# A recurrent attention kernel in which some TensorE operations are divided by columns until four steps hold exactly 2560 TensorE instructions

## The chip, the cores and the metric

The kernel runs on one core of one Trainium2 chip. The metric is the device time of one execution in microseconds, the median of several runs. A core has a matrix engine (TensorE, in the profile PE for its matmuls and PEld for its weight loads), VectorE (DVE), ScalarE (ACT), GpSimd (POOL) and SyncE (SP), which here only issues DMA. Each engine has an instruction stream of its own, and they wait for each other by semaphores.

## What is computed

Two branches over the same 2048 rows of 512 values, mixed row by row with a gate: attention that goes through the rows in 64 segments of 32 with a memory of 8 rows carried from each segment to the next, and a two-layer perceptron.

```python
for s in range(n_seg):                       # 64 segments of 32 rows
    xs = x[:, s * seg_len:(s + 1) * seg_len, :]
    h = jnp.concatenate([mem, xs], axis=1)   # 8 + 32 rows
    q = jnp.einsum('btd,dhe->bhte', h, Wq)   # 32 heads of 128
    k = jnp.einsum('btd,dhe->bhte', h, Wk)
    v = jnp.einsum('btd,dhe->bhte', h, Wv)
    scores = jnp.einsum('bhqe,bhke->bhqk', q, k) * scale
    p = softmax(where(mask, scores, -1e9))
    o = jnp.einsum('bhqk,bhke->bhqe', p, v)
    o = jnp.einsum('bhte,hed->btd', o, Wo)
    mem = o[:, :M, :]
    outs.append(o[:, M:, :])
...
h = gelu(jnp.einsum('bsd,df->bsf', layernorm(x), w1) + b1)
b = jnp.einsum('bsf,fd->bsd', h, w2) + b2
return g * a + (1 - g) * b
```

## The kernel before

A first stage of some 74 us loads the weights and computes the perceptron for all rows; for nine of the sixteen 128-row tiles its second layer is put off, and the hidden values go to DRAM. Then 64 *steps* follow, one for each segment, four to a *tile* of 128 rows (steps 0 to 3 are tile 0; `si` is the place of a step in its tile, 0 to 3). The memory makes the steps a chain: each needs the 8 rows that the one before it made.

A step on TensorE, in program order, with the lines that the profile names. A matmul of the projections has a 32-column stationary operand, so four of them stand side by side in the array and form a *group* of four; a *unit* is one such group for one of the four 128-row parts of the contraction.

- Query and key projection, 16 units of four 512-column matmuls (`qk_unit`, L128).
- Scores (L266, L270), 40 and 64 columns each, the value projection (`v_unit`, L147, 512 columns), and short sums in between (L277, L280, L701).
- `av` (L290, L295): 80 short matmuls of 40 or 64 columns.
- The output projection of the eight memory rows, `wo_pass`: eight groups of four 512-column matmuls (`wo_group`, L159).
- The new memory, `new_mem`: three blocks of 8-column matmuls (L746), each on a part of `w`, which ScalarE copies out of PSUM behind `wo_pass` (L737). VectorE then puts the result into the `hT` of the next step (L748).

In the waits of this chain TensorE does *side work* for another tile, handed out in units by a generator: `run(n)` takes the next n units of it. With `si` 0 and 1 that is the query and key projection for the last eight rows of each segment of the next tile (`left_qk`), with `si` 3 their value projection (`left_v`), with `si` 2 the output projection for such rows of the tile before (`wo_left`, eight `wo_group`s). Put-off perceptron work (L674, groups of four 256-column matmuls) is also taken in half units. In the steps with `si` 0 from tile 2 on, an output selection of two groups stands before `new_mem` (L229, L233). The numbers of units before `wo_pass`, behind it and between the blocks of `new_mem` stand in the table `WS` and in two further `run(1)`.

SyncE issues the DMA in program order. Once a step, behind `recip_x`, it writes the reciprocal sums to DRAM and reads them back as a broadcast to 128 partitions, `Rb` (512 KB); GpSimd scales the attention output with it in the next step (L730).

TensorE executes its instructions in exactly the order written (matmul, weight load and some waits each count as one). No planner moves them.

Of the kernel before, what the change touches and what calls it, by code (L numbers as in the profile page):

```python
# [28 lines left out]
def kernel(ctx, tc, A_x, A_mem0, A_Wq, A_Wk, A_Wv, A_Wo, A_seg_len, B_x, B_w1, B_b1, B_w2, B_b2, gate_w, out):  # L29
    nc = tc.nc  # L30
    P = 128
    _, S, Dm = A_x.shape
    H, Dh = A_Wq.shape[1], A_Wq.shape[2]
    M = A_mem0.shape[1]
    seg = int(A_seg_len)
    nseg = S // seg
    L = M + seg
    F = B_w1.shape[1]
    KC = Dm // P
# [22 lines left out]
    Wo_sb = pers.tile([P, H, Dm], BF16)  # L62
# [50 lines left out]
    X2 = lps.tile([P, 512], FP32)  # L113
    SbF = lps.tile([P, 512], FP32)
    W = lps.tile([P, 512], FP32)
# [5 lines left out]
    W5 = (Wq5, Wk5)  # L121
    Wv5 = Wv_sb[:].rearrange("p k (i j e) -> p k i j e", i=NG, j=4)
    HF = ((0, H // 2), (H // 2, H))

    def qk_unit(bk, G, t, hf, kc):
        h0, h1 = HF[hf]
        for j in range(4):
            nc.tensor.matmul(bk[32 * j:32 * j + 32, :], lhsT=G[:, kc, :], rhs=W5[t][:, kc, h0:h1, j, :],  # L128
                             start=(kc == 0), stop=(kc == KC - 1), tile_position=(0, 32 * j))

    def qk_cast(bk):
        Tb = ew.tile([P, 8, 32, 2], BF16, tag="Tb", bufs=3, name="Tb")
# [10 lines left out]
            nc.vector.transpose(out=dst, in_=Tb[:, jh:8:2].rearrange("p a e b -> p a (e b)").bitcast(FP32))  # L143

    def v_unit(bk, G, vb, kc):
        for j in range(4):
            nc.tensor.matmul(bk[32 * j:32 * j + 32, :], lhsT=G[:, kc, :], rhs=Wv5[:, kc, 4 * vb:4 * vb + 4, j, :],  # L147
                             start=(kc == 0), stop=(kc == KC - 1), tile_position=(0, 32 * j))

    def v_out(V, vb):  # L150
        return V[:, 4 * vb:4 * vb + 4, :].rearrange("p i e -> p (i e)")

    HORD = [(j, ih) for j in (0, 2, 1, 3) for ih in range(2)]

    def wo_group(bk, U_, n):
        j, ih = HORD[n]
        for c in range(4):
            i = 4 * ih + c
            nc.tensor.matmul(bk[32 * c:32 * c + 32, :], lhsT=U_[:, j, i, :], rhs=Wo_sb[:, 4 * i + j, :],  # L159
                             start=(n == 0), stop=(n == NW - 1), tile_position=(0, 32 * c))  # L160

    NW = len(HORD)

# [431 lines left out]
    UT = [lp.tile([P, 4, NG, 32], BF16, name=f"UT{i}") for i in range(2)]  # L595
# [14 lines left out]
    Rs = {}  # L610
    fill = iter(())

    def run(n):
        for _ in range(n):
            next(fill, None)

    def chain(*gens):
        for x in gens:
            yield from x
# [29 lines left out]
    def hm_load4():  # L649
        x = cw.tile([P, Dm], BF16, tag="c", name="c").rearrange("p (k t) -> p k t", k=KC)  # L650
        T, fc = work[0]
        nc.sync.dma_start(x[:], h_dr[T][:, fc:fc + KC])
        for k in range(KC):
            hms.append((*work.pop(0), x[:, k], 0))
# [74 lines left out]
            for h in range(2):  # L729
                nc.gpsimd.tensor_tensor(out=out[:, :, 4 * h:4 * h + 4, o:o + b - a], in0=XR[:, :, 4 * h:4 * h + 4, a:b], in1=Rb[:, h, :, :, a:b], op=ALU.mult)  # L730

    def wo_pass(U_, cuts=(0, Dm), bk=W):
        for n in range(NW):
            wo_group(bk, U_, n)
        w = cw.tile([P, Dm], BF16, tag="w", bufs=8, name="w")
        for a, b in zip(cuts, cuts[1:]):
            nc.scalar.copy(out=w[:, a:b], in_=bk[:, a:b])  # L737
        return w
# [9 lines left out]
        nc.vector.tensor_copy(out=hn[:, k0:k0 + nk, RIDE:32], in_=bk.rearrange("p (k m) -> p k m", k=nk))  # L748


    QK4 = ((0, 0), (1, 0), (0, 1), (1, 1))
    WS = ((2, 2, 1), (2, 2, 2), (2, 2, 2), (2, 2, 2))
    for s in range(nseg):
        T, si = divmod(s, SPT)
        last = s == nseg - 1
        hc, hn = hT[s % 3], hT[(s + 1) % 3]
        W1, W2, W3 = WS[si]
# [75 lines left out]
        if last:  # L833
            break
        run(W1)
        if s:
            next(mlp, None)
# [61 lines left out]
    wl, c = wls.pop(T), cs.pop(T)  # L899
# [160 lines left out]
```

## Time and profile before

| | |
|---|---|
| median of 3 runs | 754.07 us (753.94 to 754.29) |
| profiled execution, its own time | 755.67 us |
| its span in the profile | 753.8 us |
| mean granted TensorE clock | 0.998 of full |
| matmuls, and as many weight loads | 19,896 |
| TensorE instructions in a tile's four steps (tiles 2 to 14) | 609 + 601 + 601 + 601 = 2412 |

The profile's page gives the busy time and its share of the span for each engine, and a chain that is followed back from the last instruction: at each point to what released it. "issue" in that chain is time in which an engine waited for nothing that the profile shows. Matmuls overlap in the array, so the duration of one (0.38 us for 512 columns) is not its price: the price is read from how far apart groups start, as the chain of work shows it. A view by windows gives the busy time and count of each engine in stretches that one chooses; here the stretches go from the first matmul of one step to the first of another, or from inside one hole in TensorE's work to inside another. The DMA part names queues: q8 of the kind "instruction" carries instructions, not data.

### The profile page before, as it was taken

The page shows a single profiled execution, that of the slowest core. Times are in us where ns is not written, and L with a number is a line of the kernel's source. Part 1 is how long each engine was busy: PE and PEld are TensorE (multiplying, and loading weights), DVE is VectorE, ACT ScalarE, POOL GpSimd, SP SyncE. Part 2 cuts the span into 40 slices and gives each one's busy share as a digit, 9 for nine tenths or more (in the row PEclk, how much of TensorE's full clock was granted, in tenths as well). Part 3 has the DMA queues.
Part 4 walks back from the last instruction along what each step waited for, and adds up shares of the span by engine and source line. Part 5 has one row for each costly group of instructions (what it writes and reads, how often), then busy time and mean ns, then how long its engine had stood idle before and what let it go on. Part 6 is the DMA issues. An engine that isn't in the chain of part 4 may idle for free.

```text
span 753.8 us, 45384 instructions
## 1 busy us (share of the span) xinstructions
PE 736.0 (98%) x19896; PEld 429.8 (57%) x19896; DVE 399.5 (53%) x1415; ACT 535.6 (71%) x1627; POOL 274.2 (36%) x516
## 2 busy tenths in 40 slices
PE   8999999999999999999999999999999999999996
PEld 5776555555555555555555565555555655555553
DVE  6776555446454554445554545445464545555444
ACT  5777667777776776777777777767777777777663
POOL 4001323444324444334433344333443334433341
PEclk9999999999999999999999999999999999999999
DMA  9999323122321323221322313231323222222321
GB/s 312 343 335 362 104 85 87 55 76 72 93 77 46 91 70 96 69 83 53 92 77 80 86 46 93 68 96 67 70 72 86 79 72 78 57 90 74 95 70 37
DMA packets 69997, 77.17 MB, mean 102 GB/s; under 512 B 34873, under 2 KB 59938, under 8 KB 68258
## 3 DMA queue, kind: packets, MB, share of 16 engines
q1 hardware_dynamic: 68802, 72.65, 31.4%
q8 instruction: 157, 2.57, 1.4%
q0 software_dynamic: 448, 1.05, 0.5%
q10 hardware_dynamic: 544, 0.52, 0.3%
q14 instruction: 46, 0.38, 0.2%
HBM read 60.21 MB, written 7.70 MB: 90 GB/s over the span
## 4 chain that ended last, share of the span: by engine, by line
PE 91%; DVE 3%; DMA 2%; issue 2%; ACT 1%; POOL 0%; DVEq 0%; SPq 0%; ACTq 0%; POOLq 0%
PE U L128 33%; PE X L159 19%; PE X L147 17%; PE X L128 4%; PE U L290 3%; PE W L674 3%; PE U L147 2%; PE SbF L482 1%; PE U L266 1%; DMA xt<-in_A_x_dram 1%; PE W L482 1%; PE U L489 1%; DVE junk L465 1%; PE SbF L266 1%; PE SbF L701 1%
## 5 line engine op out<-in xcount | busy, mean ns | idle before, releaser
L730 POOL TENSOR_TENSOR UT<-XR,Rb 128x384 bf16<-128x384 bf16 x126 | 140.2, 1134 | 310.1 <-DMA Rb<-r_dr 252.6
L133 ACT CAST Tb<-U 128x512 bf16<-128x512 f32 x288 | 168.7, 586 | 78.7 <-PE U L128 72.5
L128 PEld LDWEIGHTS <-hT 128*32 128x32 bf16 x4096 | 108.9, 96 | 95.5 <-DVE hT L748 1.1
L147 PE MATMUL X<-Wv_sb,hT 128*32 128x512 bf16 x2048 | 144.9, 378 | 0.9 <-issue 0.9
L128 PE MATMUL U<-Wq_sb,hT 128*32 128x512 bf16 x2048 | 145.1, 380 | 0.0
L128 PE MATMUL U<-Wk_sb,hT 128*32 128x512 bf16 x2048 | 144.6, 379 | 0.0
L159 PE MATMUL X<-Wo_sb,UT 128*32 128x512 bf16 x2016 | 123.0, 380 | 0.2
L748 DVE CAST hT<-U 128x8 bf16<-128x8 f32 x126 | 21.0, 167 | 172.0 <-PE U L746 131.1
L811 ACT CAST V<-X 128x256 bf16<-128x256 f32 x256 | 88.7, 372 | 16.4 <-PE X L147 3.5
L137 DVE STREAM_TRANSPOSE QT<-Tb 128x256 f32<-128x256 f32 x128 | 57.0, 446 | 71.9 <-ACT Tb L133 71.5
L159 PEld LDWEIGHTS <-UT 128*32 128x32 bf16 x2048 | 56.6, 96 | 57.1 <-issue 17.7
L707 ACT CAST XR<-U 128x256 bf16<-128x256 f32 x252 | 78.6, 438 | 0.0
L737 ACT CAST w<-X 128x128 bf16<-128x128 f32 x189 | 44.8, 310 | 45.8 <-PE X L159 45.1
L137 DVE STREAM_TRANSPOSE KT<-Tb 128x256 f32<-128x256 f32 x128 | 57.0, 445 | 25.3 <-ACT Tb L133 25.3
L730 POOL TENSOR_TENSOR UL<-XR,Rb 128x128 bf16<-128x128 bf16 x126 | 60.2, 500 | 0.0
L147 PEld LDWEIGHTS <-hT 128*32 128x32 bf16 x2048 | 47.0, 94 | 22.3 <-issue 1.8
L842 ACT CAST UT<-U 128x64 bf16<-128x64 f32 x252 | 35.3, 227 | 28.2 <-PE U L295 28.2
L722 POOL TENSOR_TENSOR racc<-racc,R 128x72 f32<-128x72 f32 x63 | 21.2, 337 | 93.6 <-DVE R L720 49.9
L674 PE MATMUL W<-w_sb,hm 128*32 128x256 bf16 x728 | 52.7, 273 | 0.1
L794 ACT ACTIVATE E<-U 128x64 bf16<-128x64 f32 (+1 forms) x128 | 35.0, 273 | 11.3 <-PE U L270 11.1
L482 PEld LDWEIGHTS <-w_sb 128*128 128x128 bf16 (+1 forms) x352 | 33.5, 100 | 13.4 <-issue 2.4
L159 PE MATMUL X<-Wo_sb,UL 128*32 128x512 bf16 x512 | 39.8, 379 | 0.2 <-issue 0.2
(178 smaller groups left out, 1223.0 us busy)
## 6 DMA issues: line engine op xcount, KB each, us to landing
Rb<-r_dr SPq DMA_DIRECT2D x63, 512.0 KB, 3.9
Wv_sb<-in_A_Wv_dram SPq DMA_DIRECT2D x4, 1024.0 KB, 7.2
Wq_sb<-in_A_Wq_dram SPq DMA_DIRECT2D x4, 1024.0 KB, 8.5
Wk_sb<-in_A_Wk_dram SPq DMA_DIRECT2D x4, 1024.0 KB, 9.0
Wo_sb<-in_A_Wo_dram SPq DMA_DIRECT2D x4, 1024.0 KB, 9.7
VP<-VL SPq DMA_DIRECT2D x64, 64.0 KB, 3.2
hm<-h_dr SPq DMA_DIRECT2D x91, 32.0 KB, 2.2
c<-c_dr SPq DMA_DIRECT2D x16, 128.0 KB, 3.5
```

Source lines behind the costliest of these rows:

```text
L128: nc.tensor.matmul(bk[32 * j:32 * j + 32, :], lhsT=G[:, kc, :], rhs=W5[t][:, kc, h0:h1, j, :], start=(kc == 0), stop=(kc == KC - 1), tile_ ...
L133: nc.scalar.copy(out=Tb[:], in_=bk.rearrange("p (a b e) -> p a e b", a=8, b=2))
L137: nc.vector.transpose(out=dst[:, 8 * hf:8 * hf + 8, c0:c0 + 32, :].rearrange("p a r b -> p a (r b)").bitcast(FP32), in_=Tb[:].rearrange("p ...
L147: nc.tensor.matmul(bk[32 * j:32 * j + 32, :], lhsT=G[:, kc, :], rhs=Wv5[:, kc, 4 * vb:4 * vb + 4, j, :], start=(kc == 0), stop=(kc == KC - ...
L159: nc.tensor.matmul(bk[32 * c:32 * c + 32, :], lhsT=U_[:, j, i, :], rhs=Wo_sb[:, 4 * i + j, :], start=(n == 0), stop=(n == NW - 1), tile_po ...
L482: nc.tensor.matmul(hp[:rows, 0:TB * P], lhsT=w1_sb[:, kc, fc * P:fc * P + rows], rhs=yTs[blk][:, kc, :], start=(kc == 0), stop=(kc == KC - 1))
L674: nc.tensor.matmul(W[32 * c:32 * c + 32, cc], lhsT=hm[:, 32 * c:32 * c + 32], rhs=w2_sb[:, fc, cc], start=(fc == 0 and h == 0), stop=(fc = ...
L707: nc.scalar.copy(out=XR[:, j], in_=U[j][:, 0:NG * 40].rearrange("p (i q) -> p i q", q=40)[:, :, 0:32])
L730: nc.gpsimd.tensor_tensor(out=out[:, :, 4 * h:4 * h + 4, o:o + b - a], in0=XR[:, :, 4 * h:4 * h + 4, a:b], in1=Rb[:, h, :, :, a:b], op=ALU ...
L737: nc.scalar.copy(out=w[:, a:b], in_=bk[:, a:b])
L811: nc.scalar.copy(out=V[:, i0:i0 + 2, :].rearrange("p i e -> p (i e)"), in_=(X1, X2)[vb][:, 256 * h:256 * h + 256])
L842: nc.scalar.copy(out=UT[s % 2][:, j, :, 0:M], in_=U[j][:, 0:NG * 40].rearrange("p (i q) -> p i q", q=40)[:, :, 32:40])
```

## The change

`qk_unit`, `v_unit` and `wo_group` can divide each matmul by columns: `cut[0]` is 1, 2 or 4, and then each 512-column matmul becomes two of 256 or four of 128 columns, each with a weight load of its own. `wo_group` can also leave the last matmuls of its four whole (`nc4`). `run` takes a list of cuts, one for each unit, and `wo_pass` a set of groups to halve. The tables say where: in tiles 1 to 14, in the step with `si` 0, groups 4, 5 and 6 of `wo_pass` are halved and the two units between the blocks of `new_mem` are quartered; in the step with `si` 2, two of the four matmuls of group 6 are halved and the two units behind `wo_pass` and the next one are quartered. Steps 3 and 4 have entries of their own.

```diff
+    cut = [1]
+
     def qk_unit(bk, G, t, hf, kc):
-        h0, h1 = HF[hf]
-        for j in range(4):
-            nc.tensor.matmul(bk[32 * j:32 * j + 32, :], lhsT=G[:, kc, :], rhs=W5[t][:, kc, h0:h1, j, :],
-                             start=(kc == 0), stop=(kc == KC - 1), tile_position=(0, 32 * j))
+        n = H // 2 // cut[0]
+        for a in range(cut[0]):
+            h0 = HF[hf][0] + n * a
+            for j in range(4):
+                nc.tensor.matmul(bk[32 * j:32 * j + 32, 32 * n * a:32 * n * a + 32 * n], lhsT=G[:, kc, :], rhs=W5[t][:, kc, h0:h0 + n, j, :],
+                                 start=(kc == 0), stop=(kc == KC - 1), tile_position=(0, 32 * j))
...
-    def wo_group(bk, U_, n):
+    def wo_group(bk, U_, n, nc4=4):
         j, ih = HORD[n]
-        for c in range(4):
-            i = 4 * ih + c
-            nc.tensor.matmul(bk[32 * c:32 * c + 32, :], lhsT=U_[:, j, i, :], rhs=Wo_sb[:, 4 * i + j, :],
-                             start=(n == 0), stop=(n == NW - 1), tile_position=(0, 32 * c))
+        m = Dm // cut[0]
+        for a in range(cut[0]):
+            for c in range(4 if a == 0 else nc4):
+                i = 4 * ih + c
+                e = slice(m * a, m * a + m) if c < nc4 else slice(0, Dm)
+                nc.tensor.matmul(bk[32 * c:32 * c + 32, e], lhsT=U_[:, j, i, :], rhs=Wo_sb[:, 4 * i + j, e],
+                                 start=(n == 0), stop=(n == NW - 1), tile_position=(0, 32 * c))
...
-    def run(n):
-        for _ in range(n):
+    def run(n, cuts=()):
+        for k in range(n):
+            cut[0] = cuts[k] if cuts else 1
             next(fill, None)
+            cut[0] = 1
...
-    def wo_pass(U_, cuts=(0, Dm), bk=W):
+    def wo_pass(U_, cuts=(0, Dm), bk=W, halves=(), nc4=4):
         for n in range(NW):
-            wo_group(bk, U_, n)
+            cut[0] = 2 if n in halves else 1
+            wo_group(bk, U_, n, nc4 if n in halves else 4)
+            cut[0] = 1
...
+    WHP = (((4, 5, 6),), (), ((6,), 2), ())
+    UCP = ((1, 4, 4), (), (4, 4, 4), ())
+    WH = {3: ((5, 6),), 4: ((2, 3, 4, 5, 6),)}
+    UC = {3: (1, 4, 4)}
...
-        w = wo_pass(UT[s % 2], (0, P, 2 * P, Dm), X2)
+        w = wo_pass(UT[s % 2], (0, P, 2 * P, Dm), X2, *WH.get(s, WHP[si] if 4 <= s < nseg - 4 else ()))
+        uc = iter(UC.get(s, UCP[si] if 4 <= s < nseg - 4 else ()))
...
-        run(W3)
+        run(W3, [next(uc, 1) for _ in range(W3)])
...
         new_mem(w, hn, 0, si)
-        run(1)
+        run(1, [next(uc, 1)])
         new_mem(w, hn, 1, si)
-        run(1)
+        run(1, [next(uc, 1)])
```

`v_unit` is changed like `qk_unit`. In the built program a tile's four steps come to 681 + 601 + 677 + 601 = 2560 TensorE instructions in each of tiles 1 to 14, one wait a step among them; step 3 grows from 601 to 665, and the whole stream by 1076 matmuls and 1076 weight loads. The other engines' work is the same.

Two places show how TensorE's rows move. First the end of `wo_pass` in the first step of tile 2 (X is the PSUM bank of the output, UT the attention output, GL the left-over rows of the next tile). Before, its last group and the side unit behind it:

```order
L159 LDWEIGHTS UT_1364
L159 MATMUL X_123<-Wo_sb,UT_1364 32x512
...
L128 LDWEIGHTS GL
L128 MATMUL U_121<-Wk_sb,GL 32x512
...
L229 LDWEIGHTS SelR
```

and in the changed program, from a halved group on:

```order
L169 LDWEIGHTS UT_1364
L169 MATMUL X_123<-Wo_sb,UT_1364 32x256
...
L169 LDWEIGHTS UT_1364
L169 MATMUL X_123<-Wo_sb,UT_1364 32x512
...
L132 LDWEIGHTS GL
L132 MATMUL U_121<-Wk_sb,GL 32x512
```

Nothing is exchanged; the three halved groups have 24 pairs of rows for 12, the last group and the unit behind it are whole as before.

Second, the side unit between the first two blocks of `new_mem` in the same step (w is the copied output, SelM picks the memory rows). Before, four pairs of L128:

```order
L746 LDWEIGHTS w
L746 MATMUL U_118<-SelM,w 32x8
L128 LDWEIGHTS GL
L128 MATMUL U_121<-Wk_sb,GL 32x512
...
L746 LDWEIGHTS w
L746 MATMUL U_120<-SelM,w 32x8
```

and now sixteen pairs of L132:

```order
L760 LDWEIGHTS w
L760 MATMUL U_118<-SelM,w 32x8
L132 LDWEIGHTS GL
L132 MATMUL U_121<-Wk_sb,GL 32x128
...
L760 LDWEIGHTS w
L760 MATMUL U_120<-SelM,w 32x8
```

The unit stands at the same place with the same columns in all, 24 rows longer.

More of the change, by code (lines that the diff above doesn't have):

```diff
@@ L145, in v_unit @@
     def v_unit(bk, G, vb, kc):
-        for j in range(4):
-            nc.tensor.matmul(bk[32 * j:32 * j + 32, :], lhsT=G[:, kc, :], rhs=Wv5[:, kc, 4 * vb:4 * vb + 4, j, :],
-                             start=(kc == 0), stop=(kc == KC - 1), tile_position=(0, 32 * j))
+        n = 4 // cut[0]
+        for a in range(cut[0]):
+            i0 = 4 * vb + n * a
+            for j in range(4):
+                nc.tensor.matmul(bk[32 * j:32 * j + 32, Dh * n * a:Dh * n * (a + 1)], lhsT=G[:, kc, :], rhs=Wv5[:, kc, i0:i0 + n, j, :],
+                                 start=(kc == 0), stop=(kc == KC - 1), tile_position=(0, 32 * j))
     def v_out(V, vb):
@@ L153 @@
     HORD = [(j, ih) for j in (0, 2, 1, 3) for ih in range(2)]
-    def wo_group(bk, U_, n):
+    def wo_group(bk, U_, n, nc4=4):
         j, ih = HORD[n]
-        for c in range(4):
-            i = 4 * ih + c
-            nc.tensor.matmul(bk[32 * c:32 * c + 32, :], lhsT=U_[:, j, i, :], rhs=Wo_sb[:, 4 * i + j, :],
-                             start=(n == 0), stop=(n == NW - 1), tile_position=(0, 32 * c))
+        m = Dm // cut[0]
+        for a in range(cut[0]):
+            for c in range(4 if a == 0 else nc4):
[3 more added lines that the diff above has]
+                                 start=(n == 0), stop=(n == NW - 1), tile_position=(0, 32 * c))
     NW = len(HORD)
```

## The prediction

> **What bounds the kernel now.** I read the page of the profile first: busy shares, the chain that ended last, the DMA queues.
>
> ```profile
> span 753.8 us, 45384 instructions
> PE 736.0 (98%) x19896; PEld 429.8 (57%) x19896; DVE 399.5 (53%) x1415; ACT 535.6 (71%) x1627; POOL 274.2 (36%) x516
> PE 91%; DVE 3%; DMA 2%; issue 2%; ACT 1%; POOL 0%; DVEq 0%; SPq 0%; ACTq 0%; POOLq 0%
> q8 instruction: 157, 2.57, 1.4%
> Rb<-r_dr SPq DMA_DIRECT2D x63, 512.0 KB, 3.9
> ```
>
> TensorE is the bound: 98% busy, 91% of the chain. So whatever shortens the time must take out TensorE work or the few holes in it, and 2% of the chain, some 15 us, is "issue": TensorE waits for nothing that the profile shows. The fourth line names a suspect. 39,792 matmuls and weight loads over 157 packets is 253 instructions to a packet, of 2.57 MB / 157 = 16.4 KB: queue 8 brings TensorE's instructions, in blocks of about 256.
>
> Next I looked along the chain for the pieces called issue, and counted TensorE's instructions from inside one hole to inside another. (Columns of the chain: start, length, what. Of the windows: stretch, length, then busy time and count of each engine, the granted clock, the DMA share, GB/s.)
>
> ```profile
> 207.55 0.02 PE U L290 x4
> 207.57 0.69 issue
> 208.26 0.25 PE U L290 x12
> ...
> 292.26 0.77 issue
> ...
> 323.66 0.59 issue
> ...
> 500.67 1.00 issue
> ...
> 541.66 0.03 PE U L280 x4
> 541.68 0.20 issue
> ...
> 709.62 0.52 issue
> ```
>
> ```profile
> 207.70:292.50 84.80, 83.68 (x2428) 47.24 (x2428) 43.68 (x154) 61.30 (x195) 33.27 (x60) 1.00 0.25 75
> 292.50:323.90 31.40, 30.63 (x895) 17.84 (x894) 15.95 (x58) 22.18 (x68) 11.80 (x21) 1.00 0.22 67
> 323.90:500.90 177.00, 175.62 (x5111) 100.93 (x5112) 89.96 (x320) 129.22 (x404) 70.16 (x124) 1.00 0.27 78
> 500.90:709.80 208.90, 207.10 (x6006) 119.88 (x6006) 107.34 (x378) 151.92 (x475) 81.93 (x144) 1.00 0.26 76
> L159 PEldq EVENT_SEMAPHORE x63: 51/51/51, 81.9 to 731.2; - x63
> ```
>
> The last row says that each of the 63 steps has one further TensorE instruction, a wait. With it the four stretches hold 2428+2428+8 = 4864, 895+894+3 = 1792, 5111+5112+17 = 10,240 and 6006+6006+20 = 12,032 instructions: 19, 7, 40 and 47 times 256, to the last one. The holes lie at the ends of instruction blocks. A block's end does not always cost: there are 155 of them and far fewer holes. Counted from the first instruction of their step, the six above stand at about 417, 457, 438, 429, 321 and 401, that is in the 160 short instructions of `av` (L290, L295), just behind them, or behind the short ones of L277 and L280. Block ends in the long 512-column streams leave no mark.
>
> The size of all this comes from steps with no mark, one for each place in a tile, against all of tiles 1 to 14 (steps 4 to 59).
>
> ```profile
> 661.35:671.82 10.47, 10.47 (x317) 5.95 (x312) 4.79 (x18) 7.94 (x25) 4.03 (x7) 1.00 0.36 114
> 338.16:348.32 10.16, 10.16 (x304) 6.00 (x296) 5.96 (x20) 7.46 (x25) 4.06 (x7) 1.00 0.28 77
> 306.57:316.74 10.17, 10.17 (x313) 5.71 (x305) 5.50 (x20) 7.49 (x24) 4.07 (x7) 1.00 0.28 87
> 441.82:451.99 10.17, 10.17 (x313) 5.73 (x305) 5.29 (x18) 7.43 (x24) 4.36 (x8) 1.00 0.12 33
> sum 40.97, PE 40.97 PEld 23.40 DVE 21.54 ACT 30.32 POOL 16.52; mean PE 10.24 PEld 5.85 DVE 5.39 ACT 7.58 POOL 4.13
> ...
> 118.25:702.94 584.69, 579.32 (x16860) 332.08 (x16853) 299.36 (x1056) 425.39 (x1331) 229.97 (x405) 1.00 0.26 76
> 159.71:200.79 41.08, 41.08 (x1216) 23.51 (x1209) 21.36 (x76) 30.35 (x96) 16.45 (x29) 1.00 0.29 83
> 284.89:327.69 42.80, 41.44 (x1216) 23.78 (x1209) 20.88 (x75) 30.41 (x96) 16.49 (x29) 1.00 0.27 80
> ```
>
> A tile without holes takes 40.97 us; tile 2 came near it (41.08), tile 5 lost 1.8 us. Tile 1 has no output selection (two groups of four, 0.22 each as priced below), so 14 tiles would take 13 x 40.97 + 40.53 = 573.1 us. They took 584.7. **11.6 us** are lost at block ends there: what the change can win at most in these tiles.
>
> **The change, part by part.** A tile now has 2412 TensorE instructions, 108 more than nine blocks, so block ends wander from tile to tile and meet every place in turn. With 2560, ten blocks, they stay put. Counted in the changed program, they stand at about 41, 297, 553 of a tile's first step, 128, 384 of the second, 39, 295, 551 of the third and 130, 386 of the fourth, in each of tiles 1 to 14; step 3's own additions bring them there. None is in the second half of `av` or behind it. 384 and 386 are in the short sums and the first group of `av`; the others stand in or just behind long streams. So by the map of the holes the 11.6 us go. The edge steps (0 to 3, 60 to 63) keep holes of their own; I take them as unchanged.
>
> What it adds: 1076 matmuls and their weight loads, with the same columns in all. There are 72 side units in quarters (2 a tile in the first step, 3 in the third, 2 in step 3), 46 output groups in halves, and 14 groups with half of their four split. Prices are from these pieces of the chain:
>
> ```profile
> 668.12 0.16 PE U L290 x16
> 668.31 0.55 PE X L128 x8
> 668.85 1.75 PE X L159 x32
> 541.52 0.11 PE W L674 x4
> 671.24 0.02 PE U L746 x3
> ```
>
> Eight groups of four 512-column matmuls take 1.75 us, 0.219 a group; a group of four 256-column ones 0.11; so two halves cost 0.22, as before: 46 x 0 to 0.005, 0.1 us. A quarter group, four of 128 columns, is not in the trace. Below it cannot be less than a quarter of 0.219, 0.055, or the unit costs nothing more; above, it could be as slow as the 256-column group, 0.11, and a unit then 0.44, +0.22. Much narrower groups pass in 0.02 to 0.04 (four of L290 in 0.16/4, three of L746 in 0.02), so the issue of four pairs is no floor at 0.055, and I take 0.057 on the line through 0.11 and 0.219: +0.01 a unit, 0.6 us for 72. Together **+0.7 us** (bounds 0 and 16). All of it is on the path, TensorE being the bound; no casts, loads or queue entries move, and the ScalarE copies of `w` that the side units cover get a little more cover.
>
> What may stay. Each block is fetched by DMA while the one before it runs, so a block must run longer than its fetch is late. DMA load within a step, in a step without holes and the start of the next:
>
> ```profile
> 306.57:309.07 2.50, 2.50 (x60) 1.29 (x56) 1.99 (x8) 1.92 (x4) 0.00 (x0) 1.00 0.69 225
> 309.07:311.57 2.50, 2.50 (x104) 1.39 (x96) 1.41 (x4) 1.79 (x5) 2.41 (x3) 1.00 0.03 5
> 311.57:314.07 2.50, 2.50 (x114) 1.55 (x102) 1.94 (x8) 1.91 (x11) 1.08 (x4) 1.00 0.03 7
> 314.07:315.57 1.50, 1.50 (x32) 0.83 (x28) 0.00 (x0) 1.16 (x5) 0.59 (x3) 1.00 0.19 34
> 315.57:316.74 1.17, 1.17 (x45) 0.66 (x33) 0.17 (x1) 0.71 (x3) 0.00 (x0) 1.00 0.56 212
> 316.74:319.24 2.50, 2.50 (x60) 1.29 (x56) 1.05 (x5) 1.66 (x3) 0.54 (x1) 1.00 0.32 125
> ```
>
> The engines are busy from a step's last microsecond into the next one's third: the 512 KB broadcast `Rb` (3.9 us). A fetch that falls in there is late. The hole at 541.68 is of that kind: its block began 65 instructions into its step, and the boundary cost 0.20 us there. Of the new blocks four begin around a broadcast: at 553 and 551, and at 41 and 39. The first two are also made shorter in time: of their 256 instructions 48 and some 58 are additions that bring no work with them, so each ends earlier by what as many others would have taken. I allow one hole of 0.20 us a tile there, **2.8 us** for 14; from below 0, from above two such holes, 5.6.
>
> Sum: 11.6 - 0.7 - 2.8 = 8.1 us less. Against the profiled execution: span 753.8 to 745.7, and its time of 755.67 to 747.6. The profiled one lies 1.6 above the median of the runs, 754.07, so for the runs **746.0 us**.
>
> The Trainium skill, "Runtime: NRT & Kernel Launch", section "Instruction fetch mechanics", says that instructions come in 16 KiB blocks of 256, and the trace agrees (253, counts to the last one). It adds that crossing a block's end is mostly hidden; by that rule there would be nothing to win and 0.7 us to lose. The trace has holes up to 1.00 us there, so the measurement decides for those places.
>
> **Rivals.**
>
> *The fixed places are bad ones (slower).* What is paid, is then paid in all 14 tiles. The likeliest are 384 and 386, some 15 instructions ahead of the earliest hole in `av` that I saw (401, 0.52 us). If each cost what the hole at 207.57 did, 0.69: 28 x 0.69 = 19.3 us back, 754.1 - 11.6 + 0.7 + 19.3 = 762.5. It decides from 10.9 / 28 = 0.39 us a boundary on. Against it: the blocks that end there begin at 128 and 130, in the long streams and after the broadcast's worst. One such place alone, 14 x 0.69 = 9.7, would leave 752.9.
>
> *Narrow matmuls have a floor (slower).* At 0.11 for a group of 128 columns, 72 x 0.22 = 15.8 us: 754.1 - 11.6 + 0.1 + 15.8 + 2.8 = 761. It decides from 0.15 us a unit on. Against it stand the rows of L290 and L746.
> The Trainium skill, "TensorE: Matmul & The Clock Gate", section "Wait — 56ns, not 53.3ns?", has a floor of about 25 ns from start to start; by it sixteen matmuls take 0.40, which speaks for this rival. Sixteen of L290 in 0.16 us go against it for matmuls on separate parts of the array, which the quarters are.
>
> *The counts don't hold.* If the executed stream has instructions that I can't count, block ends still wander; with ten blocks for 9.4 there would be as many holes and a few more: 754.1 + 0.7 + 0.06 x 11.6 = 755.5. The four exact multiples of 256 speak against it.
>
> *The time turns up elsewhere.* Without holes the ScalarE and VectorE chain between `w` and the next step's `hT` could end last in some steps. In the four steps without holes TensorE was busy throughout, so I see no such wait; if half the gain went there, 750.
>
> **How the numbers follow.** Forecast, with 0 to 0.4 us of holes left in a tile: 0.66. Bad places: 0.15, half of it with one place only or part of a hole (faster or the same still, about 750 to 754), half slower. Floor: 0.06. Counts: 0.06. Elsewhere: 0.07. The low end is all holes gone and no cost left in the edge steps, 754.1 - 11.6 + 0.7 less some 0.3: 742.9. The high end takes in the time that turns up elsewhere and one bad place short of its whole price: 751.5. A measurement of this kernel tells 0.2%, 1.5 us, from no change. Faster by more than that: 0.66 + 0.07 + most of the first half of the bad places, 0.80. Within it 0.05. Slower 0.15: the other bad places, the floor, and part of the counts.
>
> **What would show it.** Right: tiles 1 to 14 of 41.0 to 41.4 us each, all alike, where they now range from 41.08 to 42.80; issue pieces in the chain gone there, those of the edge steps still there; quarter units of 0.22 to 0.24 us in the chain; PE near 99%; queue 8 with some 8 packets more. Wrong: an issue piece, or a stretched group, at the same place in every tile, above all around `av` of the second and fourth step or early in the second and fourth step, where the blocks from 553 and 551 end; quarter units of 0.3 us and more; holes that still wander.

## The result and the profile after

The changed kernel takes **760.91 us** (median of 7 runs, 758.48 to 763.64), the one before 754.29 in 7 runs (749.22 to 754.43): 1.0103 times as long, 95% interval 1.0077 to 1.0129. The forecast was 746.0, with a range to 751.5. The change makes the kernel slower, by about 1%.

The page of the changed kernel's profiled execution (762.34 us), the lines that answer to those shown of before:

```profile
span 760.5 us, 47528 instructions
PE 736.5 (97%) x20964; PEld 437.2 (57%) x20972; DVE 397.2 (52%) x1415; ACT 536.3 (71%) x1627; POOL 274.3 (36%) x516
PE 90%; DMA 3%; DVE 3%; issue 2%; ACT 1%; SPq 0%; DVEq 0%; ACTq 0%
q8 instruction: 165, 2.70, 1.5%
Rb<-r_dr SPq DMA_DIRECT2D x63, 512.0 KB, 3.8
```

TensorE's busy time is what it was (736.0), the span is 6.7 us longer, and queue 8 has the eight packets more that were foretold. So TensorE does not work longer, it stands longer. Windows of the same profile, first all of tiles 1 to 14, then the four steps of tile 10, then two steps with `si` 3:

```profile
118.44:710.00 591.56, 581.74 (x17897) 339.76 (x17892) 297.30 (x1058) 426.00 (x1331) 230.06 (x405) 1.00 0.25 76
499.14:509.62 10.48, 10.48 (x344) 6.39 (x340) 4.83 (x18) 7.68 (x25) 4.05 (x7) 1.00 0.30 88
509.62:520.42 10.80, 10.52 (x304) 5.82 (x300) 5.91 (x22) 7.73 (x25) 4.05 (x7) 1.00 0.25 83
520.42:530.63 10.21, 10.21 (x342) 6.18 (x338) 5.54 (x21) 7.38 (x24) 4.08 (x7) 1.00 0.08 22
530.63:540.80 10.17, 10.17 (x304) 5.75 (x300) 5.25 (x19) 7.57 (x25) 4.32 (x8) 1.00 0.22 73
...
487.53:499.14 11.61, 10.53 (x304) 5.87 (x300) 4.64 (x18) 7.71 (x25) 4.30 (x8) 1.00 0.25 73
615.59:625.76 10.17, 10.17 (x304) 5.71 (x300) 5.25 (x19) 7.57 (x25) 4.32 (x8) 1.00 0.17 48
```

The 14 tiles take 591.56 us where they took 584.69: +6.87, all of the difference. The reader is to see that the steps with additions (`si` 0 and 2) are not the slow ones. They run without a hole at 10.48 and 10.21; those with `si` 1 and 3, which hold the same instructions as before, take 10.17 where nothing is late, and up to 11.61. Hole-free, a tile is 10.48 + 10.17 + 10.21 + 10.17 = 41.03 us; with 0.44 less in tile 1, which has no output selection, 14 tiles are 574.0. So **17.6 us** are lost at block ends, where 11.6 were before. By steps, as the time beyond the quickest with the same `si`, `si` 1 and 3 lost 6.7 and 8.9, 0 and 2 only 1.2 and 0.6. By places, the ends at 384 and 386 lost 10.2 us and those at 128 and 130 5.7, from the start times of the single matmuls there.

The chain of work through the slow step that starts at 487.53 shows where (start, length, what):

```profile
490.72 0.01 PE SbF L276
490.73 0.28 issue
491.02 0.28 PE SbF L276 x13
...
494.08 0.17 PE U L300 x9
494.25 0.79 issue
495.05 0.22 PE U L300 x7
```

and the same two places of the hole-free one that starts at 615.59, in its chain:

```profile
618.79 0.10 PE SbF L276 x15
618.88 0.03 PE SbF L280 x3
...
621.68 0.20 PE U L300 x16
621.88 0.04 PE U L305 x4
```

The first hole is at instruction 130 of the step, the second at 386: two of the ten fixed ends. The waits of TensorE say how often, over the whole execution (us in total, times, the longest):

```profile
PE U L300 <- issue: 7.4, 19, 0.8
PE SbF L276 <- issue: 2.2, 7, 0.5
```

Much of what they miss of the 17.6 is pieces that are stretched and not empty, like the 13 matmuls above that took 0.28 us where fifteen take 0.10.

Why two fetches are late can be read from the DMA part, asked for short windows: 2.5 us from the moment when the block that began at instruction 551 was entered (486.2), the next 2.5 us, and the same start of the block ahead of the hole-free step (614.2).

```profile
DMA packets 183, 0.53 MB, mean 213 GB/s; under 512 B 55, under 2 KB 55, under 8 KB 183
q1 hardware_dynamic: 183, 0.53, 64.7%
```

```profile
DMA packets 3, 0.02 MB, mean 7 GB/s; under 512 B 2, under 2 KB 2, under 8 KB 2
q8 instruction: 1, 0.02, 2.4%
q1 hardware_dynamic: 2, 0.00, 0.0%
```

```profile
q1 hardware_dynamic: 137, 0.50, 53.4%
q8 instruction: 1, 0.02, 4.4%
```

In the late case the broadcast `Rb`, nearly all of these 0.53 MB, goes first and no packet of queue 8 among it; that comes when it is through, 2.56 us after the block was entered. In the other case it gets in among its first packets, at 0.09. (Entries of blocks are good to about 0.1 us: eight matmul records are missing in the first stage of this trace, and because of them the windows and entries here lie eight matmuls behind the true first one.) From the single packets and matmuls of this trace, for tiles 2 to 13, a step with `si` 2 and the next one (us; "late" is the start of the fetch after the entry of the block, "lost" the time of the instructions around a block's end beyond the quickest):

| fetch sent at 551, late | lost at 130 | fetch sent at 130, late | lost at 386 |
|---|---|---|---|
| -0.04 | 0.00 | -0.89 | 0.00 |
| 0.02 | 0.00 | 0.15 | 0.00 |
| 0.09 | 0.00 | -0.03 | 0.00 |
| 2.01 | 0.00 | 0.89 | 0.34 |
| 2.16 | 0.20 | 1.05 | 0.42 |
| 2.23 | 0.32 | 1.05 | 0.44 |
| 2.37 | 0.36 | 1.09 | 0.45 |
| 2.44 | 0.52 | 1.05 | 0.43 |
| 2.48 | 0.42 | 1.32 | 0.69 |
| 2.56 | 0.47 | 1.10 | 0.98 |
| 2.66 | 0.56 | 1.06 | 0.70 |
| 2.81 | 0.72 | 1.09 | 0.43 |

The block from 551 to 130 runs 4.42 us without a hole (614.25 to 618.67), that from 130 to 386 only 3.06 (618.67 to 621.73). Where a fetch was waited for, the block that it brought ran 4.42 - late + lost = 2.3 to 2.5 us after its start at 130, and 3.06 - late + lost = 2.4 to 2.9 us at 386. So the first block bears a fetch that is 2.0 late, and the second, by the sum, one of about 0.6 (0.15 cost nothing, 0.89 cost 0.34). A fetch that starts before its block is entered has a lead, as the one at -0.89; behind a hole, or a hole hardly avoided, that lead is gone, and the next fetch starts 0.9 to 1.3 late. So one late fetch makes two holes. The table shows that they go together; that the broadcast makes the first is tested below.

### The profile page after: what moved, and what is told of

Read it like the earlier page. It is cut to its first block, busy times and chain, and to the rows that moved or that the text cites. A ratio compares the mean times of both kernels' runs of the same rounds, so it can differ in the third digit from the quotient of the medians.

```text
span 760.5 us, 47528 instructions
## 1 busy us (share of the span) xinstructions
PE 736.5 (97%) x20964; PEld 437.2 (57%) x20972; DVE 397.2 (52%) x1415; ACT 536.3 (71%) x1627; POOL 274.3 (36%) x516
## 3 DMA queue, kind: packets, MB, share of 16 engines
q0 software_dynamic: 448, 1.05, 0.5%
## 4 chain that ended last, share of the span: by engine, by line
PE 90%; DMA 3%; DVE 3%; issue 2%; ACT 1%; SPq 0%; DVEq 0%; ACTq 0%
PE U L132 33%; PE X L169 18%; PE X L154 17%; PE X L132 4%; PE U L300 3%; PE W L686 3%; PE U L154 2%; PE U L276 1%; PE SbF L276 1%; DMA w_sb<-in_B_w_dram 1%; DMA xt<-in_A_x_dram 1%; PE SbF L492 1%; DVE junk L475 1%; PE W L492 1%; PE SbF L713 1%
## 5 line engine op out<-in xcount | busy, mean ns | idle before, releaser
L132 PEld LDWEIGHTS <-hT 128*32 128x32 bf16 x4096 | 107.5, 96 | 97.1 <-DVE hT L762 1.1
L132 PE MATMUL U<-Wq_sb,hT 128*32 128x512 bf16 x2048 | 144.8, 380 | 0.0
L132 PE MATMUL U<-Wk_sb,hT 128*32 128x512 bf16 x2048 | 144.2, 379 | 0.0
L169 PE MATMUL X<-Wo_sb,UT 128*32 128x512 bf16 (+1 forms) x2228 | 120.7, 360 | 0.0
L169 PEld LDWEIGHTS <-UT 128*32 128x32 bf16 x2260 | 61.6, 96 | 54.2 <-issue 12.4
L154 PEld LDWEIGHTS <-hT 128*32 128x32 bf16 x2048 | 46.6, 94 | 21.4 <-issue 0.6
L276 PEld LDWEIGHTS <-KT 128*32 128x32 bf16 x2048 | 28.5, 95 | 20.4 <-issue 8.2
```

Source lines behind the costliest of these rows:

```text
L132: nc.tensor.matmul(bk[32 * j:32 * j + 32, 32 * n * a:32 * n * a + 32 * n], lhsT=G[:, kc, :], rhs=W5[t][:, kc, h0:h0 + n, j, :], start=(kc ...
L154: nc.tensor.matmul(bk[32 * j:32 * j + 32, Dh * n * a:Dh * n * (a + 1)], lhsT=G[:, kc, :], rhs=Wv5[:, kc, i0:i0 + n, j, :], start=(kc == 0) ...
L169: nc.tensor.matmul(bk[32 * c:32 * c + 32, e], lhsT=U_[:, j, i, :], rhs=Wo_sb[:, 4 * i + j, e], start=(n == 0), stop=(n == NW - 1), tile_po ...
L276: nc.tensor.matmul(Sb[i2][32 * j:32 * j + 32, i - 4 * i2, M:M + 40], lhsT=KT[:, h // 2, :, h % 2], rhs=QT[:, h // 2, :, h % 2], start=Fals ...
```

## The experiments

Theory A: the broadcast makes fetches late, and fixed block ends pay for it where two of ten blocks begin beside it. Theory B: fixed ends are good or bad by place alone. Theory C: the added instructions cost by themselves, since each block runs a shorter time. The runs were made in five sets on different chips. On each the kernel before ran beside them, and took 754.1 (places, 32 partitions), 751.7 (bf16, early additions), 754.6 (64 partitions, drift, late broadcast), 750.1 (drift and moved places with 32 partitions, first halves) and 755.1 us (second halves). Ratios are to it, and kernels of one set are compared best.

**Other places.** More additions ahead of tile 1 move all fixed ends, by 48 and by 224.

```diff
-    WH = {3: ((5, 6),), 4: ((2, 3, 4, 5, 6),)}
+    WH = {1: ((1, 2),), 3: ((1, 2, 3, 4, 5, 6),), 4: ((2, 3, 4, 5, 6),)}
```

> The changed kernel with 24 more matmul pairs (48 TensorE instructions) ahead of the periodic tiles, by halving six more groups of the output projection in steps 1 and 3. The period stays 2560; every block end of tiles 1 to 14 now stands 48 instructions earlier in its step: at about 249 and 505 with si 0, 80, 336 and 592 with si 1, 247 and 503 with si 2, 82, 338 and 594 with si 3. Theory (it is the phase: blocks whose fetch is asked for late in a step queue behind the broadcast, are late at their end, and the lost lead makes the next one late too): the blocks from 503 and 505 are asked for before the broadcast and the short chain 129, 385 is gone, so tiles of 41.0 to 41.2 us and about 743 to 746 us in all. Rival (divided matmuls or more blocks cost time wherever they stand): 760 to 761 as before. Rival (any fixed place is as bad as another): 754 to 762.

> The same with 224 instead of 48 instructions added ahead of the periodic tiles (groups halved in steps 0 to 3 and two side units quartered in step 0), so block ends stand at about 73, 329, 585 with si 0, 160, 416 with si 1, 71, 327, 583 with si 2, 162, 418 with si 3. Phase theory: with fetches asked for at 583 and 585, behind the broadcast, and ends at 416 and 418 within the short attention matmuls, holes of some 1.9 us a tile, 770 us (764 to 777). Rival (cost of dividing): 761. Rival (any fixed place alike): 754 to 762.

Measured: 764.98 us by 48 (761.46 to 768.83; ratio to before 1.0147, 1.0108 to 1.0187), a miss, and 773.93 by 224 (ratio 1.0253, 1.0207 to 1.0299), as expected. In the first case most of the loss moved with the ends, to 80 and 82 of the second and fourth step (11 of the 17 us found at ends), behind fetches from 503 and 505 that are 0.5 to 2.9 us late. These places are in the long streams of the projection, L132, where the prediction had seen no mark:

```profile
PE U L132 <- issue: 7.3, 11, 0.9
```

So a place outside of the short matmuls is not enough. Whether the places are bad without the broadcast too, as B has it, the next runs decide.

**A shorter broadcast.** `Rb` is read into 32 partitions only; the other 96 are scaled by 1, so this kernel leaves out a part of the work, and only its time is of use.

```diff
+    Rbp = lp.tile([P, P, NG], FP32)
...
+    nc.gpsimd.memset(Rbp[:], 1.0)
...
-        Rb = cw.tile([P, P, NG], FP32, tag="Rb", bufs=1, name="Rb")
+        Rb = Rbp
...
-        nc.sync.dma_start(Rb[:].rearrange("p r e -> p (r e)"), r_dr[s % 2][:].rearrange("r e -> (r e)").partition_broadcast(P))
+        nc.sync.dma_start(Rb[0:32].rearrange("p r e -> p (r e)"), r_dr[s % 2][:].rearrange("r e -> (r e)").partition_broadcast(32))
```

> The changed kernel with the broadcast Rb cut from 128 to 32 partitions (128 KB instead of 512 KB); the other 96 partitions of the attention output are scaled by 1 instead of by their reciprocal sums, all else is done. Phase theory, with the broadcast as what makes the fetches of 551 and 553 late: the holes at 129 and 131 go, and with them those at 385 and 387, which only follow from the lost lead: 743 to 746 us, tiles of 41.0 to 41.2. Rival (the blocks from 129 to 385 and from 131 to 387 are too short in themselves): the holes at 385 and 387 stay, some 0.35 us each and 10 us in all, 752 to 756. Rival (cost of dividing): 761.

> The kernel before with the same shorter broadcast (the other 96 partitions scaled by 1). How much of its 11.6 us of holes comes from fetches behind the broadcast, and how much from blocks that are short in themselves around the attention matmuls. If the broadcast makes most of them: 744 to 748 us. If it makes only those at about 320 of a step and its like: 750 to 753.

Measured: the changed kernel 748.24 us (747.12 to 749.16; ratio to the whole kernel before 0.9904, 0.9874 to 0.9933), the one before 750.86 (0.9951, 0.9929 to 0.9974). The first is above the 743 to 746 of the theory and below the 752 of its rival, the second in the lesser of its two cases. Tiles 1 to 14 of the changed one, by windows and by TensorE's waits for issue:

```profile
119.94:696.67 576.73, 576.30 (x17897) 344.27 (x17896) 300.65 (x1058) 425.43 (x1331) 230.65 (x405) 1.00 0.15 39
```

```profile
PE U L300 <- issue: 0.4, 1, 0.4
```

and of the one before:

```profile
119.34:697.23 577.89, 576.32 (x16852) 331.46 (x16852) 299.31 (x1058) 425.19 (x1331) 230.18 (x405) 1.00 0.15 38
```

The broadcast makes 591.56 - 576.73 = 14.8 of the 17.6 us. Both holes of a pair went, though nothing was changed at 384/386: nothing is lost there now, and 1.1 us at 128 and 130. Nor does it come at a kinder time: its packets start 9.6 us into a step (median), where they started at 9.2. So B, the place alone, falls here. It also made a part of the 11.6 us of before: 584.69 - 577.89 = 6.8 by the tiles of the two profiled executions, of which one lies above its median and the other below, and 754.1 - 750.9 = 3.3 by the medians. A is shown for the changed kernel; of the losses before, it is a part. With 64 partitions:

> The changed kernel with the broadcast Rb read into 64 of the 128 partitions only (256 KB; the other 64 are scaled by 1). Theory (a fetch of instructions that stands behind the packets of the broadcast is late by what of them is left): between the kernel with 32 partitions (748.2) and the changed one (760.9), 752 to 756 us, with holes at 128/130 that are about half as long. Rival (it is not the length of the broadcast but that there is one at that time): 759 to 762. If half the packets are already enough to let the fetches through: 748 to 750.

750.61 us (ratio 0.9939, 0.992 to 0.9958), tiles 578.56: with half the packets the tiles lose 578.56 - 574.0 = 4.6 us for 17.6. The time is below the range of the theory and nearest to the last sentence of the expectation.

**Do the additions cost by themselves?** The table is thinned to 2520 instructions a tile, so that the ends drift again.

```diff
-    WHP = (((4, 5, 6),), (), ((6,), 2), ())
-    UCP = ((1, 4, 4), (), (4, 4, 4), ())
+    WHP = (((5,),), (), ((6,), 2), ())
+    UCP = ((1, 4, 1), (), (4, 4, 4), ())
```

> The changed kernel with 40 fewer additions in each of tiles 1 to 14: in the steps with si 0 only group 5 of wo_pass is halved and only one unit between the blocks of new_mem is quartered. A tile holds 2520 TensorE instructions, so the ends of the blocks move by 40 from tile to tile and meet every place in turn; the other splits stay, and the broadcast is whole. Theory (the additions shorten the time that a block of 256 runs, so that more fetches come late at whatever place the ends stand): 1.2 to 1.5 us of holes a tile, 757 to 763 us. Rival (only the unlucky fixed places of the changed kernel cost, and wandering ends cost what they cost before): 0.8 us of holes a tile, 754 to 756 us.

> The drifting kernel of 2520 instructions a tile (761.1) with the broadcast read into 32 partitions only (the other 96 scaled by 1). Theory (short blocks cost through the late broadcast fetches and by having less lead in av): more than the kernel before with 32 partitions (750.9), 752 to 756. Rival (the additions cost only where the broadcast is late): 750 to 752.

> The changed kernel with all places of the block ends moved by 48 (765.0 with the whole broadcast), and with the broadcast read into 32 partitions only (the other 96 scaled by 1). Theory (the broadcast is the whole cause of what a fixed place costs): 747 to 751. Rival (the places are bad by themselves, having short blocks behind them): 755 to 763.

Measured: 761.10 us with drift and the whole broadcast (760.6 to 768.18; 1.0092, 1.0055 to 1.013), 750.71 with drift and 32 partitions (1.0015, 0.9995 to 1.0036), 746.97 with the places moved by 48 and 32 partitions (0.9958, 0.9946 to 0.9971). The first is in the range of C, the second in that of C's rival, the third at the low end of what A says; the moved places, 765.0 with the whole broadcast, lose only 577.42 - 574.0 = 3.4 us in tiles 1 to 14 with the short one, which starts at nearly the same time (9.2 us into a step for 9.3). Tiles 1 to 14 of the drifting one with the whole broadcast, and with 32 partitions, by windows:

```profile
118.71:715.00 596.29, 582.11 (x17624) 337.91 (x17620) 297.52 (x1058) 425.73 (x1331) 229.84 (x405) 1.00 0.26 75
```

```profile
118.71:699.34 580.63, 577.97 (x17624) 341.23 (x17624) 299.25 (x1058) 425.38 (x1331) 230.89 (x405) 1.00 0.14 38
```

The profiled execution of the first was its slowest (768.18 us), so its tiles are long by some 7 us. The four tables:

| block ends | whole broadcast: us, ratio | 32 partitions: us, ratio |
|---|---|---|
| before, 2412 a tile, wandering | 750.1 to 755.1, 1 | 750.9, 0.9951 |
| 2520 a tile, drifting | 761.1, 1.0092 | 750.7, 1.0015 |
| 2560, fixed as in the change | 760.9, 1.0103 | 748.2, 0.9904 |
| 2560, fixed and moved by 48 | 765.0, 1.0147 | 747.0, 0.9958 |

In the second column fixed ends gain: 750.9 - 748.2 = 2.6 us in one set, 750.7 - 747.0 = 3.7 in the other. In the first they gain nothing. C is not settled. With the whole broadcast the additions cost 761.1 - 754.6 = 6.5 us even where the ends drift; with the short one nothing by the medians (750.7 and 750.9), 580.63 - 577.89 = 2.7 us by the tiles of the two profiled executions, and up to 0.6% by the ratios, which were taken on two chips. That the additions cost where they shorten the very blocks that begin beside the broadcast would fit, and was not tried by itself.

**Can the fetches be let through with all the work done?** First fewer bytes: reciprocals and `Rb` in bf16, 256 KB, with a second reciprocal on VectorE.

```diff
...
+            nc.vector.reciprocal(out=Rh[:], in_=xs8)
...
-        Rb = cw.tile([P, P, NG], FP32, tag="Rb", bufs=1, name="Rb")
-        nc.sync.dma_start(r_dr[s % 2][:], R[:, 8 * NG:RW])
+        Rb = cw.tile([P, P, NG], BF16, tag="Rb", bufs=1, name="Rb")
+        nc.sync.dma_start(r_dr[s % 2][:], Rh[:])
```

> The changed kernel with the broadcast Rb in bf16 (256 KB instead of 512 KB, one small VectorE operation more a step); nothing is left out. Theory (fetches of the blocks from 551 and 553 queue behind the broadcast): between the changed kernel and the run with 128 KB, the fetches start about 1 us earlier, which is more than the mean hole: 746 to 750 us. Rival (it was the number of DMA packets, which stays, and not their bytes): 758 to 762.

> The kernel before with the broadcast in bf16. Theory: between 750.9 (128 KB) and 754.1 (512 KB), so 751 to 753 us. Rival (packets, not bytes): 754 to 755.

781.15 us for the changed kernel (1.04, 1.036 to 1.0439), 759.64 for the one before (1.0098, 1.0075 to 1.0121): both missed, and upwards. The DMA part of the changed one has the transfer as long from issue to landing as with twice the bytes:

```profile
Rb<-r_dr SPq DMA_DIRECT2D x63, 256.0 KB, 3.9
hm<-h_dr SPq DMA_DIRECT2D x91, 32.0 KB, 3.5
```

Its packets are as many, and the loads beside it got slower (`hm` has 1.9 in the changed kernel). It is no test of the bytes alone, though: the packets also start later, 10.6 us into a step (median) for 9.2, and now the blocks that end at 39 and 41 lose too, 12.6 us in all where they lost 0.1. How much of the later start is the second reciprocal, and how much the transfers, stays open.

Second, the additions put early in the steps, all in groups 1 to 6 of `wo_pass` (quarters and halves), so that the block ends lie elsewhere, with the broadcast whole and in bf16:

```diff
...
-    WHP = (((4, 5, 6),), (), ((6,), 2), ())
-    UCP = ((1, 4, 4), (), (4, 4, 4), ())
...
+    Q4, H2 = (4, 4), (2, 4)
+    WPP = ({1: Q4, 3: H2, 4: Q4, 5: H2, 6: (2, 2)}, {}, {1: Q4, 3: H2, 4: Q4, 5: Q4}, {})
...
```

> The same period of 2560 with all additions moved: 148 TensorE instructions a tile, now by halving and quartering groups 1 to 6 of the output projection in the steps with si 0 and si 2 alone; the side units behind it are whole again. The blocks whose fetch falls into the broadcast are then not shortened. Block ends stand at about 25, 281, 537 with si 0, 116, 372 with si 1, 27, 283, 539 with si 2, 114, 370 with si 3; the broadcast has its full size. Theory (a block must run as long as its fetch is late plus 2.4 us; the changed kernel shortens the two blocks that have the latest fetch): the blocks from 537 and 539 run about 5.2 and 4.9 us, which covers most fetches; holes of 0 to 0.5 us a tile, 743 to 751 us. Rival (any fixed phase loses, since the fetch at its late place is paid in each tile, shortened or not): 757 to 765. Rival (quartered groups cost by themselves): 760.

> The moved additions and the bf16 broadcast together. Theory: next to no holes left in tiles 1 to 14, 742 to 746 us, the fastest of all. Rival (any fixed phase loses): 752 to 760.

766.58 (1.019, 1.0168 to 1.0213) and 768.12 (1.0222, 1.0201 to 1.0243), both missed. With the whole broadcast the fetches from 537 mostly start 2.4 to 3.5 us late and those from 25 and 27 mostly 2.0 to 3.0. The broadcast's packets start at 10.2 us of their step (median) where they start at 9.2 in the changed kernel, so the places were moved and the broadcast with them. A fetch now falls on the time of the write of the reciprocals; that this is what delays the broadcast was not tested.

Third, the broadcast later, behind a ScalarE copy of the reciprocals that stands after its casts of `UT`. It was meant to be 1.2 us; the packets start 0.8 us later in the changed kernel (median):

```diff
...
+    def bcast(s, R):
+        Rc = cx.tile([P, NG], FP32, tag="Rc", name="Rc")
+        nc.scalar.copy(out=Rc[:], in_=R[:, 8 * NG:RW])
+        Rb = cw.tile([P, P, NG], FP32, tag="Rb", bufs=1, name="Rb")
+        nc.sync.dma_start(r_dr[s % 2][:], Rc[:])
+        nc.sync.dma_start(Rb[:].rearrange("p r e -> p (r e)"), r_dr[s % 2][:].rearrange("r e -> (r e)").partition_broadcast(P))
...
+        bcast(s, R)
         x_raw(s)
```

> The changed kernel with the write of the reciprocal sums and the broadcast Rb, whole as before, put about 1.2 us later: ScalarE copies the reciprocals behind its casts of UT, and the two transfers wait for that copy. Theory (the fetches that are sent for when the blocks from 551 and 553 begin are late because they stand behind the packets of the broadcast): they get ahead of it, the holes at 128/130 go, with them those at 384/386, and the time is 745 to 752 us, below both kernels. Rival (the later broadcast meets the fetches at 39 and 41 of the next steps in the same way, or the scaling of the attention output is late): 758 us or more.

> The kernel before with the same later broadcast, as the control: block ends wander over all places, and a broadcast at another time meets as many of them: 752 to 757 us. If it comes out below 750, the later broadcast is better whatever the places of the block ends.

The changed kernel takes 755.20 us so (749.39 to 759.57 in 10 runs; 1.0014, 0.9984 to 1.0044), the one before 762.49 (1.0092, 1.0056 to 1.0128). Tiles 1 to 14, changed and before:

```profile
119.44:701.67 582.23, 579.74 (x17896) 341.18 (x17892) 300.67 (x1058) 430.31 (x1387) 229.76 (x405) 1.00 0.26 76
```

```profile
120.24:710.26 590.02, 581.29 (x16852) 333.44 (x16848) 307.02 (x1058) 430.36 (x1387) 229.16 (x405) 1.00 0.27 75
```

For the changed kernel, theory and rival are both half right; the control missed its range. The fetches from 551 and 553 mostly got ahead, and the holes behind them nearly went: the steps with `si` 1 and 3 lose 1.6 and 1.3 us in all for 6.7 and 8.9. But those from 39 are now 0.7 to 2.4 us late, and the steps with `si` 2 lose 4.1. With ends that wander, the later broadcast costs 8 us; with fixed ones the ratio falls from 1.0103 to 1.0014. The transfer is the same, so where the ends stand against it decides.

Fourth, the broadcast in two halves of 64 partitions. With the second issued by ScalarE:

```diff
...
+        rb_half(nc.scalar, s, Rbs[s], 64)
         x_raw(s)
```

> The changed kernel with the whole broadcast Rb in two halves of 64 partitions: the first at its old place on SyncE's queue, the second issued by ScalarE behind its casts of UT, about 1 us later. Theory (a fetch is late by the packets of the broadcast that stand ahead of it without a break): a fetch waits for one half at most, as with 64 partitions alone (750.6), the holes at 128/130 and 384/386 go, and the time is 749 to 754. Rival (what counts is how many packets there are in all, or the second half meets the fetches instead): 757 to 762. The issue of the second half takes some of ScalarE's time in each step, off the path of the end.

> The kernel before with the broadcast in the same two halves, as the control. With places that wander, two shorter stretches of packets meet more fetches and delay each less: 750 to 757. If it is as fast as the changed kernel with halves, fixed places bring nothing.

836.64 us (1.116, 1.1114 to 1.1205) and 832.14 (1.1084, 1.1034 to 1.1134): a mistake in the experiment. The expectation says that the issue is off the path, and the waits of ScalarE in the changed one say otherwise:

```profile
ACT XR L719 <- DMA r_dr<-R: 67.1, 36, 3.0
```

ScalarE waits for the write of the reciprocals before it can issue the second half, and its own work stands behind that. So again, both halves on SyncE's queue, the second behind a small copy that sets its time:

```diff
...
+        nc.scalar.copy(out=Rbs[s][64:P, 0, :], in_=R[64:P, 8 * NG:RW])
+        rb_half(s, Rbs[s], 64)
         x_raw(s)
```

> The changed kernel with the whole broadcast in two halves of 64 partitions, both on SyncE's queue; the second waits for a copy of 8 values that ScalarE makes behind its casts of UT, and so comes about 1 us behind the first. No engine but SyncE waits for a transfer here. Theory (a fetch is late by the packets that stand ahead of it without a break): 748 to 754, below the changed kernel by 7 to 12. Rival (all packets of the broadcast count, or the second half meets the fetches as the whole one did): 757 to 762.

> The kernel before with the same two halves on SyncE's queue, as the control: 750 to 757 by the theory, and, whatever the halves are worth, above the changed kernel with halves if fixed places gain once the fetches get through.

761.35 us (1.0082, 1.0052 to 1.0113), the rival, and 759.22 (1.0064, 1.0044 to 1.0083), a miss. The tiles of the changed kernel lose about as much as with the whole broadcast, but elsewhere: 7.2 us with `si` 1 and 3 for 15.6, 9.1 with 0 and 2 for 1.8. Not only the split differs: the first packets start about 1.1 us later in the step than in the changed kernel (median), and the last ones end 1.4 later (13.34 us from its start for 11.94). No kernel that does all the work was faster than the one before; the later broadcast with fixed ends is level with it. In all five tries in the changed kernel that kept the work on SyncE's queue (bf16, the two with early additions, the later broadcast, these halves) the packets start 10.0 to 10.6 us into a step, so a shorter or divided broadcast at the old time, with all the work done, was not tried.

## Why the prediction was wrong

**Right:** that queue 8 brings TensorE's instructions in blocks of 256 and that the holes are at their ends; that 2560 holds in the executed stream, with every end at the counted place; that TensorE is the bound and the edge steps stay as they were (the span outside of tiles 1 to 14 is 168.9 us, before 169.1). The split was priced right: 0.22 to 0.24 us for a quarter unit was foretold, and the chain of the changed kernel has 0.23 (it shows 14 of the 16 matmuls; the trace has all of them):

```profile
508.60 0.02 PE U L760 x3
508.62 0.23 PE U L132 x14
508.84 0.02 PE U L760 x3
```

A hole-free tile is 41.03 us for 40.97, 0.8 us in 14, against +0.7. The rival of the narrow floor (0.44 a unit) falls with it. No wait on `w` or `hT` took the gain either.

**Wrong: the step "What may stay".** It named the cause and the blocks (those that begin at 551 and 553, beside the broadcast, shortened by additions), and sized them at one hole of 0.20 us a tile, 2.8 us, 5.6 at most. It is 17.6 us, 1.26 a tile. The difference of 14.8 us is the miss (760.9 - 746.0 = 14.9). Two things were wrong in it.

- The price was taken from the one hole of before whose block began beside the broadcast, 0.20 us. That fetch was late in a block of the usual length. What the step lacked is the sum that decides: a fetch behind the whole broadcast starts 2.0 to 2.8 us late and takes about 2.4 more, against 4.42 us that the block runs. That is 0 to 0.8 us of hole, in most tiles.
- It took each block by itself. A late fetch leaves the next one without its lead, and the next block, to 384 or 386, runs only 3.06 us: a second hole, mostly the longer one. With that, the first rival (384 and 386 as bad places, 762.5) named the dearer of the two places, but not the cause: they cost 10.2 us and not 19.3, with 5.7 at 128 and 130 beside them, and nothing (with 1.1 beside them) once the broadcast is short. That its time came so near is luck. The argument against it, that the blocks which end there begin after the broadcast's worst, was the mistake; they begin after a hole that the broadcast made.

The Trainium skill, "Runtime: NRT & Kernel Launch", section "Instruction fetch mechanics", calls a crossing mostly hidden; by it the change would have cost 0.7 us. The two lines of the waits above, 26 waits of up to 0.8 us at `av` and the scores, go against it for blocks beside a large transfer.

The noise was taken too small as well: 1.5 us from three runs, where seven spread over 5.2. It decides nothing here, the miss being 14.9.

**The gain** was also taken too high, though it did not decide. Of the 11.6 us of before, 3.3 to 6.8 come from the broadcast and are not cured by fixing the ends, only moved. Where the broadcast is short, fixing them is worth the 2.6 and 3.7 us above: the sign of the forecast, a third to a half of its 8.1.

## What to carry to other kernels

Where instruction blocks end at a fixed place, ask of each block how long it runs, how late its successor's fetch can start behind the transfers of that time, and what the fetch takes; and ask it of the block behind as well, since here a hole handed its lateness on. Look at the large transfer before the instruction count: here a broadcast into a quarter of the partitions was worth 13 to 15 us in the changed kernel (760.9 to 748.2; ratio 1.0103 to 0.9904), and none of the tables of splits that were tried gained while it stood.

## What the runs showed that was not expected

- The fetches of instructions waited behind data here: with 0.53 MB, nearly all of it the broadcast, under way, none of queue 8 was served for 2.56 us; the packet then took 0.024 x 16 x 2.5 = 0.96 us of one engine.
- Half the bytes in as many packets hardly made the broadcast shorter, half the packets did. From the start of its first packet to the end of its last it takes 2.4 us in the changed kernel (medians), 2.1 in bf16, 1.7 with 64 partitions, 0.9 with 32. The time from issue to landing shows this badly: 3.8 us, 3.9, 3.7, and with 32 partitions

```profile
Rbp<-r_dr SPq DMA_DIRECT2D x63, 128.0 KB, 2.5
```

- Whether a fetch gets ahead of the broadcast varies from tile to tile with the same program and the same places: in the table above from -0.04 to 2.81. That this is also what spreads the runs is not shown: the runs of the changed kernel spread over 5.2 us and with 32 partitions over 2.0, but those of the drifting kernel with 32 partitions over 5.7.
